# Transposing DMA transfers for the second layer's keys of three heads, in place of turning them on TensorE

## The chip, the cores and the metric

One core of one Trainium2 chip. The metric is the device time of the whole kernel in microseconds (us). Runs of one kernel lie within about 0.8% here; a verdict of "faster" or "slower" needs 2%. A ratio is the mean time of one kernel's fast runs over the mean of the other's fast runs of the same rounds, so it is not quite the ratio of the medians that are quoted. Profiles are single executions. The runs below were made in three batches, each on another chip and beside before, whose medians there were 1132.5, 1131.1 and 1134.4 us; a difference between runs of two batches is good to a few us only.

## The reference, cut to what matters

Two identical layers of cached attention and an MLP, for 8 batch rows with one new token each. Each layer reads the same caches.

```python
def _A_ref(x, k_cache, v_cache, wq, wo):          # caches: (8, 8, 4096, 256), bf16
    q = (x @ wq).reshape(B, 1, 16, 256)...        # 16 query heads on 8 key heads
    scores = einsum("bhqd,bhkd->bhqk", q, k) * 256 ** -0.5
    o = einsum("bhqk,bhkd->bhqd", softmax(scores), v)
    return o... @ wo
x = x + _A_ref(_layernorm(x), ...)    # layer 1
x = x + _B_ref(_layernorm(x), ...)    # MLP
x = x + _A_ref(_layernorm(x), ...)    # layer 2, the same caches
x = x + _B_ref(_layernorm(x), ...)
```

One head of one batch row has 2 MB of keys and 2 MB of values. A score needs the sum over the 256 dimensions. The kernel's matmuls take the keys with the dimensions on the partitions, and the cache has them the other way round: the keys have to be turned (transposed).

## The kernel before

A small planner in the kernel, run when the kernel is built, orders all work over the engines and issues all loads on one queue, that of SyncE (SP). SBUF holds 30 quarters of 512 KB for keys and values. Of each batch row the keys of five "kept" heads stay in SBUF from layer 1 to layer 2; the three "free" heads (0, 1, 2) are loaded and turned again in layer 2. That makes 64 + 24 = 88 fresh key heads.

A load, four quarters at most, and the turning of half a quarter on TensorE, pairs of bf16 taken as one f32, with the eviction back into the same place:

```python
src = cache[b, h].rearrange("(m s) d -> m (s d)", m=P)[:, u * 2048:(u + n) * 2048]
dst = kv[:, q * 2048:(q + n) * 2048]
o.emit = lambda eng: eng.dma_start(dst, src)
# ... cut ...
def transpose_piece(i, pc):
    # ... 4 transposes of 128x128 f32 into a PSUM bank ...
    last = t.transpose(psT[bank][:, s * P:(s + 1) * P], src, ident_f[:, :])
    # ... then one copy back by VectorE or ScalarE, whichever the planner picks
```

After it the key of pair c (even or odd dimensions) lies at every second element, and the queries are made for even and odd dimensions to match:

```python
w = wq_sb[:, kc, hq * 256 + c:hq * 256 + 256:2]          # queries
a = slot_ap(q, s * 256, 256)                             # scores, 16 per quarter
last = t.matmul(ps[:, 2 * i:2 * i + 2 * REP], a[:, c:256:2], bcast(rhs(c), REP, 1), ...)
```

The planner's constants for a load are its rate and `ISSUE`, the time from issue to its start.

Of the kernel before, what the change touches and what calls it, by code (L numbers as in the profile page):

```python
# [6 lines left out]
P = 128  # L7
# [16 lines left out]
REP = 24  # L24
AT = (-4, -3, -2)
MLP_AT = 3
MIX = "KKKKKFFF"
QFIRST = 1
PV0 = 0
PV1 = PV0 + DH  # L30
QW, HW, YW = 24, 24, 12
SC = 448
# [30 lines left out]
class Plan:  # L63
# [3 lines left out]
    WIN, COLS, TARGET = 3.413, 3000, 3500  # L67


    ISSUE, LEAD = 3.5, 6.0  # L70
    BLOCK, FETCH = 128, 6.0
    LAT = {"pe": 0.25, "dve": 0.06, "act": 0.06, "pool": 0.05, "sp": 0.4}

# [364 lines left out]
def bass_interleave_layers__gqa_block_cached__mixer_s_mlp__decode_kernel(  # L438
# [38 lines left out]
    wq_sb = sb("wq_sb", [P, 3, 4096], bf)  # L477
# [86 lines left out]


    FASTER = 1.05

    def dma(name, dst, src, nbytes, sem, val, wr, at, row=8192):

# [11 lines left out]

    def issue_kv(o, n, q):

        (cache, b, h), u = o.unit.tile, o.unit.u
        src = cache[b, h].rearrange("(m s) d -> m (s d)", m=P)[:, u * 2048:(u + n) * 2048]
        dst = kv[:, q * 2048:(q + n) * 2048]
        slot_n[q] += 1
        o.emit = lambda eng: eng.dma_start(dst, src)
        o.dma = (slot_sem[q], 16 * slot_n[q])
        o.dur = ((n << 15) / 26.88e3 + 8 * 0.008) / FASTER  # L590

    plan.issue_kv = issue_kv

    def load(cache, b, h, units, keep=()):

        out = {}
        tile = (cache, b, h)
        for u in units:
            x = out[u] = Unit(tile, u, u in keep)
            o = plan.op("sp", None, 0.0, "kv", wr=[("s", x, 0), ("s", x, 1)], prio=loads[0])  # L600
            o.unit = x
            loads[0] += 1
        return out
# [54 lines left out]
    def pe(fn, n, rd=(), wr=(), banks=(), name="chain", prio=None, pairs=None):  # L658
        if prio is None:
            prio = urge[0] + len(plan.ops)  # L660
        d = 0.06 + 0.026 * n
        return plan.op("pe", fn, (d, d, 20 * n, pairs or n), name, rd=rd, wr=wr, banks=banks, prio=prio)
# [86 lines left out]
               rd=["xc", "rsy"], wr=["base"])  # L749
            dv(lambda v: v.tensor_tensor(bs, bs, src, ALU.add), rd=["base", skey], wr=["base"])  # L750

    def q_mms(t, mts, rhs, bank, at, step, copies):



        last = None
        for i, mt in enumerate(mts):
            hq, c = mt // 2, mt % 2
            for kc in range(4):


                if kc < 3:
                    w = wq_sb[:, kc, hq * 256 + c:hq * 256 + 256:2]
                    r = rhs(kc)
                else:
                    o = (hq % 8) * 256
                    w = wqx_sb[:, o + c:o + 256:2]
                    r = rhs(3 + hq // 8)
                if step == 1:
                    r = bcast(r, copies, 1)  # L770
                last = t.matmul(bank[:, at + i * step:at + i * step + copies], w, r,  # L771
                                start=(kc == 0), stop=(kc == 3))
        return last
# [20 lines left out]
    def column_sums():  # L794

        def one(kc):
            return mask[:, kc:kc + 1]
        for g in range(4):
            pe(lambda t, g=g: q_mms(t, range(8 * g, 8 * g + 8), one, psM, SC, 1, QW), 32,
               rd=["mask"] + WQ, wr=["psM"], banks=[M], prio=len(plan.ops))  # L800

            dv(lambda v, g=g: v.tensor_copy(
                cs_q[:, 8 * g:8 * g + 8].rearrange("p (h c j) -> p h c j", c=2, j=2),
                psM[:, SC:SC + 8].rearrange("p (h j c) -> p h c j", c=2, j=2)),
               rd=["psM"], wr=["cs_q"], banks=[M], prio=len(plan.ops))
        pe(lambda t: h_mms(t, one, psM, SC, 1, HW), 56, rd=["mask"] + W3, wr=["psM"], banks=[M],
           prio=len(plan.ops))
        dv(lambda v: v.tensor_copy(cs_h[:, :], psM[:, SC:SC + 14]), rd=["psM"], wr=["cs_h"], banks=[M],
           prio=len(plan.ops))
# [72 lines left out]
    def front(layer, b, h):  # L882


        g = fronts[0]
        fronts[0] += 1
        par, nr, nm = 0, free_p.pop(0), g % NS
        ps, bk = psS, "S"
        kept_k, kept_v = state.pop((0, b, h)) if layer else ({}, {})
        keep_k = KEPT_K.get(h, ()) if layer == 0 else ()  # L890
        if layer == 0:
            def rhs(c):
                return q1T[:, b, 4 * h + 2 * c:4 * h + 2 * c + 2]
            qk = [("q1T", 0), ("q1T", 1)]
        else:
            def rhs(c):
                return q2T[b % 2][:, 4 * h + 2 * c:4 * h + 2 * c + 2]
            qk = [("q2", b, h)]
        ks = dict(kept_k)
        fresh = [u for u in range(4) if u not in ks]  # L900
        ks.update(load(A_k_cache, b, h, fresh, keep_k))
        for u in range(4):
            if u in fresh:
                for pc in range(2):
                    transpose_piece(ks[u], pc)

            def sc(t, u=u, q=ks[u]):
                last = None
                for s in range(8):
                    i = 8 * u + s  # L910


                    for c in range(2):
                        a = slot_ap(q, s * 256, 256)
                        last = t.matmul(ps[:, 2 * i:2 * i + 2 * REP], a[:, c:256:2],  # L915
                                        bcast(rhs(c), REP, 1), start=(c == 0), stop=(c == 1))
                return last
            o = plan.op("pe", sc, (0.022 * 16 + 0.06, 32 * REP / 1200 + 0.01, 32 * REP, 16), "sc",
                    rd=qk + [("s", ks[u], 0), ("s", ks[u], 1)],
                    wr=[("sc", par, x) for x in range(u, 4)], banks=[bk])  # L920
            if u not in keep_k:
                o.frees = ks[u]
        hi = len(plan.ops) - 10 ** 5
        scs = [("sc", par, x) for x in range(4)]

        ss = sS[nm]
        plan.op("dve", lambda v: v.tensor_copy(ss[:, :], ps[:, 0:64]), 0.17, "max", rd=scs,  # L927
                wr=[("sS", nm)], banks=[bk], prio=hi)
        sview = ss[:, :].rearrange("p (i j) -> p j i", j=2)
        plan.op("dve", lambda v: v.tensor_reduce(pm[nm][:, :], sview, axis=AX.X, op=ALU.max), 0.23,  # L930
                "max", rd=[("sS", nm)], wr=[("pm", nm)], prio=hi)
        plan.op("pool", lambda gp: gp.partition_all_reduce(gm[nm][:, :], pm[nm][:, :], P, RO.max),  # L932
                0.46, "max", rd=[("pm", nm)], wr=[("gm", nm)], prio=hi)
        plan.op("dve", lambda v: v.tensor_single_scalar(nb[nm][:, :], gm[nm][:, :], -INV_SQRT_DH,  # L934
                                                        ALU.mult), 0.15, "max",
                rd=[("gm", nm)], wr=[("nb", nm)], prio=hi)

        for jj in range(2):
            def ex(a, jj=jj):
                return a.activation(pT[nr][:, :, :].rearrange("p i j -> p j i")[:, jj, :],  # L940
                                    sview[:, jj, :], ACT.Exp, bias=nb[nm][:, jj:jj + 1],
                                    scale=INV_SQRT_DH, accum_out=rs[nr][:, jj:jj + 1])
            plan.op("act", ex, 0.5, "exp", rd=[("nb", nm), ("sS", nm)], wr=[("pT", nr, jj), ("rs", nr, jj)], prio=hi)
        plan.op("pool", lambda gp: gp.partition_all_reduce(Db[nr][:, :], rs[nr][:, :], P, RO.add),  # L944
                0.5, "sum", rd=[("rs", nr, 0), ("rs", nr, 1)], wr=[("Db", nr)], prio=hi)
        plan.op("dve", lambda v: v.reciprocal(rc[nr][:, :], Db[nr][:, :]), 0.15, "sum",
                rd=[("Db", nr)], wr=[("rc", nr)], prio=hi)
        state[layer, b, h] = ({u: ks[u] for u in keep_k}, kept_v, nr)
# [160 lines left out]
    def second_queries(b, h, prio):  # L1109

        q, src = q2T[b % 2], x2c[b % 2]
        pe(lambda t: q_mms(t, range(4 * h, 4 * h + 4), lambda kc: src[:, kc, 0:1], psM, SC,
                           1, QW), 16, rd=[("x2", b)] + WQ, wr=["psM"], banks=[M], prio=prio)
        dv(lambda v: v.scalar_tensor_tensor(
            q[:, 4 * h:4 * h + 4].rearrange("p (c j) -> p c j", c=2),
            psM[:, SC:SC + 4].rearrange("p (j c) -> p c j", c=2), rsy[:, 0, 0:1],
            t_q[:, 4 * h:4 * h + 4].rearrange("p (c j) -> p c j", c=2), ALU.mult, ALU.add),
           rd=["psM", "rsy", "t_q"], wr=[("q2", b, h)], banks=[M], prio=prio)
# [25 lines left out]
    def first_queries():  # L1144
# [9 lines left out]
           banks=[M])  # L1154
        norm(xT[:, :, :], "xT", False)
        for h in range(8):
            pe(lambda t, h=h: q_mms(t, range(4 * h, 4 * h + 4), lambda kc: yb[:, kc, :], psM,
                                    32 * h, B, B), 16, rd=YB + WQ, wr=["psM"], banks=[M])
        for c in range(2):
            dv(lambda v, c=c: v.tensor_copy(  # L1160
# [129 lines left out]
```

## Time and profile before

| | us |
|---|---|
| median of 3 runs | 1135.38 (1130.73 to 1138.06) |
| profiled span | 1124.7 |
| bytes from HBM | 446.8 MB |

Lines of the page of before: busy time by engine, GB/s in 40 equal slices of the span, the kernel's DMA queue (packets, MB, share of 16 engines' span), the chain that ended last, and the groups that turn and evict keys (line, engine, operation, tiles, count, busy us, mean ns of one, idle before and what ended it):

```profile
PE 959.9 (85%) x19455; PEld 771.8 (69%) x19455; DVE 556.0 (49%) x1749; ACT 275.8 (25%) x839; POOL 98.0 (9%) x273
GB/s 334 408 424 421 389 397 424 422 421 382 419 425 423 415 379 422 423 425 408 393 425 423 421 387 409 423 425 420 371 412 426 424 417 374 426 420 398 365 336 132
q1 hardware_dynamic: 59392, 446.80, 97.5%
...
PE 53%; DMA 35%; DVE 5%; issue 5%; SPq 1%; POOL 0%; ACT 0%
...
L1067 PE MATMUL psT<-ident_f,kv 128*128 128x128 f32 x2816 | 398.4, 288 | 32.1 <-DMA kv<-in_A_k_cache_dram 28.9
L1075 DVE COPY kv<-psT 128x512 f32<-128x512 f32 x388 | 267.1, 691 | 214.9 <-PE psT L1067 213.9
L1076 ACT COPY kv<-psT 128x512 f32<-128x512 f32 x316 | 184.9, 586 | 407.6 <-PE psT L1067 407.6
```

Three stretches of before by window (start and end in us, length, busy time and count of each engine (PE, its weight loads, VectorE, ScalarE, GpSimd), granted TensorE clock as a share of full speed, busy share of the DMA engines, GB/s): normal streaming, one batch row's MLP chain, and the tail.

```profile
169.00:253.00 84.00, 75.27 (x1298) 63.80 (x1297) 44.00 (x112) 29.33 (x81) 7.96 (x21) 0.94 1.00 422
267.00:281.00 14.00, 10.78 (x263) 6.69 (x261) 7.41 (x42) 0.21 (x1) 0.00 (x0) 0.98 0.97 352
1054.00:1110.00 56.00, 46.88 (x1072) 39.01 (x1069) 25.77 (x94) 11.83 (x43) 6.05 (x16) 0.88 0.90 331
```

How to read it: in the long stretch the DMA engines are busy all the time and deliver 422 GB/s; TensorE is busy 75 of 84 us, close behind. At 424 GB/s the traffic alone takes 449.5 MB / 424 GB/s = 1060 us. The remaining 65 us are the head, a dip in each batch row (352 GB/s here, where the MLP's serial chain runs and loads come in quarters) and the tail. The chain gives TensorE 53%: both are loaded, and the chain alone doesn't tell which one sets the rate.

### The profile page before, as it was taken

How to read it: one execution, taken by the hardware profiler on the slowest of the kernel's cores; microseconds unless marked ns; L12 is line 12 of the kernel's file. 1: busy time of each engine (PE TensorE's matmuls, PEld its weight loads, DVE VectorE, ACT ScalarE, POOL GpSimd, SP SyncE). 2: the span in 40 equal slices, each digit the busy share in tenths (PEclk: the TensorE clock that was granted, in tenths of full speed). 3: DMA queues.
4: the chain of work that ended last, by engine and by line, in shares of the span. 5: the costliest groups of instructions: out<-in, count | busy, mean ns of one | idle time of the engine just before them, and what ended most of it. 6: DMA issues, size and time to landing. Idle time of an engine off the chain costs nothing.

```text
span 1124.7 us, 42351 instructions
## 1 busy us (share of the span) xinstructions
PE 959.9 (85%) x19455; PEld 771.8 (69%) x19455; DVE 556.0 (49%) x1749; ACT 275.8 (25%) x839; POOL 98.0 (9%) x273
## 2 busy tenths in 40 slices
PE   5888888898789989798898987989878988898887
PEld 4677557785678757687677855777666975676775
DVE  4345435455365544454455543655534554456444
ACT  1133012341123302243023411233012430132120
POOL 0001010010100101010010101001010010110010
PEclk9899899899899999999899998899999999999888
DMA  9999999999999999999999999999999999999993
GB/s 334 408 424 421 389 397 424 422 421 382 419 425 423 415 379 422 423 425 408 393 425 423 421 387 409 423 425 420 371 412 426 424 417 374 426 420 398 365 336 132
DMA packets 59570, 449.50 MB, mean 400 GB/s; under 512 B 6384, under 2 KB 9600, under 8 KB 34688
## 3 DMA queue, kind: packets, MB, share of 16 engines
q1 hardware_dynamic: 59392, 446.80, 97.5%
q8 instruction: 152, 2.49, 0.9%
q14 instruction: 26, 0.21, 0.0%
HBM read 446.77 MB, written 0.01 MB: 397 GB/s over the span
## 4 chain that ended last, share of the span: by engine, by line
PE 53%; DMA 35%; DVE 5%; issue 5%; SPq 1%; POOL 0%; ACT 0%
DMA kv<-in_A_k_cache_dram 23%; PE psT L1067 21%; PE psS L915 15%; DMA kv<-in_A_v_cache_dram 11%; PE psP L970 8%; PE psR L1017 3%; PE psM L771 2%; PE psT L1231 1%; DVE oS L982 1%; DVE oS L984 1%; DMA w3x_sb<-in_B_w_dram 1%; PE psP L992 1%; PE psM L868 1%; PE psM L871 1%; SPq L571 1%
## 5 line engine op out<-in xcount | busy, mean ns | idle before, releaser
L1067 PE MATMUL psT<-ident_f,kv 128*128 128x128 f32 x2816 | 398.4, 288 | 32.1 <-DMA kv<-in_A_k_cache_dram 28.9
L1075 DVE COPY kv<-psT 128x512 f32<-128x512 f32 x388 | 267.1, 691 | 214.9 <-PE psT L1067 213.9
L1067 PEld LDWEIGHTS psT<-ident_f,kv 128*128 128x128 f32 x2816 | 320.2, 147 | 54.2 <-DMA kv<-in_A_k_cache_dram 35.4
L1076 ACT COPY kv<-psT 128x512 f32<-128x512 f32 x316 | 184.9, 586 | 407.6 <-PE psT L1067 407.6
L970 PE MATMUL psP<-kv,pT 128*2 128x256 bf16 x4096 | 168.2, 278 | 26.0 <-DMA kv<-in_A_v_cache_dram 15.1
L940 ACT ACTIVATE pT<-sS,nb 128x32 bf16<-128x32 f32 x256 | 81.7, 326 | 332.1 <-DVE nb L934 332.0
L915 PE MATMUL psS<-q2T,kv 128*128 128x48 bf16 x4096 | 141.9, 187 | 20.2 <-issue 19.3
L915 PEld LDWEIGHTS psS<-q2T,kv 128*128 128x128 bf16 x4096 | 126.3, 99 | 44.0 <-issue 39.4
L915 PEld LDWEIGHTS psS<-q1T,kv 128*128 128x128 bf16 x4096 | 136.9, 98 | 14.4 <-issue 9.6
L915 PE MATMUL psS<-q1T,kv 128*128 128x48 bf16 x4096 | 145.7, 184 | 0.9 <-issue 0.9
L970 PEld LDWEIGHTS psP<-kv,pT 128*2 128x2 bf16 x4096 | 79.2, 82 | 63.9 <-issue 25.9
L932 POOL PARTITION_ALL_REDUCE gm<-pm x128 | 45.6, 356 | 792.2 <-DVE pm L930 792.2
L927 DVE COPY sS<-psS 128x64 f32<-128x64 f32 x128 | 28.7, 224 | 120.7 <-PE psS L915 116.3
L992 PE MATMUL psP<-sel,oS 128*128 128x2 bf16 x512 | 32.2, 166 | 48.6 <-DVE oS L984 44.0
L982 DVE CAST oS<-psP 128x256 bf16<-128x256 f32 x128 | 53.9, 421 | 38.7 <-PE psP L970 35.6
L992 PEld LDWEIGHTS psP<-sel,oS 128*128 128x128 bf16 x512 | 24.4, 99 | 68.4 <-DVE oS L984 62.8
L1017 PE MATMUL psR<-wo_sb,oT 128*1 128x448 bf16 x448 | 65.4, 375 | 5.1 <-DVE oT L998 4.9
L944 POOL PARTITION_ALL_REDUCE Db<-rs x128 | 51.2, 400 | 202.2 <-ACT pT L940 202.2
L984 DVE TENSOR_TENSOR oS<-psP,oS 128x256 bf16<-128x256 f32 x128 | 54.2, 423 | 3.2
L1231 PE MATMUL psT<-ident_b 128*128 128x512 bf16 x162 | 54.4, 416 | 0.0
L940 ACT ACTIVATION_READ_ACCUMULATOR pT<-sS,nb 128x1 f32 x256 | 48.1, 188 | 0.0
L771 PEld LDWEIGHTS psM<-x2c,wq_sb 128*128 128x128 bf16 x768 | 30.3, 98 | 21.7 <-issue 17.1
(126 smaller groups left out, 505.7 us busy)
## 6 DMA issues: line engine op xcount, KB each, us to landing
kv<-in_A_k_cache_dram SPq DMA_DIRECT2D x71, 2048.0 KB, 21.7
kv<-in_A_v_cache_dram SPq DMA_DIRECT2D x51, 2048.0 KB, 19.2
kv<-in_A_v_cache_dram SPq DMA_DIRECT2D x171, 512.0 KB, 7.6
kv<-in_A_v_cache_dram SPq DMA_DIRECT2D x42, 1024.0 KB, 12.1
kv<-in_A_k_cache_dram SPq DMA_DIRECT2D x9, 1536.0 KB, 16.0
kv<-in_A_v_cache_dram SPq DMA_DIRECT2D x7, 1536.0 KB, 15.0
kv<-in_A_k_cache_dram SPq DMA_DIRECT2D x21, 512.0 KB, 8.8
kv<-in_A_k_cache_dram SPq DMA_DIRECT2D x10, 1024.0 KB, 14.5
```

The source lines that it names most:

```text
L771: last = t.matmul(bank[:, at + i * step:at + i * step + copies], w, r, start=(kc == 0), stop=(kc == 3))
L915: last = t.matmul(ps[:, 2 * i:2 * i + 2 * REP], a[:, c:256:2], bcast(rhs(c), REP, 1), start=(c == 0), stop=(c == 1))
L940: return a.activation(pT[nr][:, :, :].rearrange("p i j -> p j i")[:, jj, :], sview[:, jj, :], ACT.Exp, bias=nb[nm][:, jj:jj + 1], scale=IN ...
L970: last = t.matmul(ps[g4:g4 + 2, PV0:PV0 + DH], pT[nr][:, i, :], slot_ap(q, s * 256, 256), start=(i < 4), stop=(i >= 28), skip_group_check= ...
L982: plan.op("dve", lambda v: v.tensor_copy(oS[:, 0, :], po), 0.36, "o", rd=[("pv", par, x) for x in range(4)], wr=["oS0"], banks=[bk], prio=hi)
L984: plan.op("dve", lambda v: v.tensor_tensor(oS[:, 1, :], po, oS[:, 0, :], ALU.subtract), 0.36, "o", rd=["oS0"] + [("pv", par, x) for x in r ...
L992: last = t.matmul(ps[:, PV1 + 2 * c:PV1 + 2 * c + 2], oS[:, w, c:DH:2], sel[:, :], start=(w == 0), stop=(w == 1))
L1017: last = t.matmul(psR[r:r + 1, 0:D], oT[no][:, i % 2, i // 2:i // 2 + 1], wo_sb[:, a:a + D], start=(k == 1 and i < 2), stop=(k == HKV - 1 ...
L1067: last = t.transpose(psT[bank][:, s * P:(s + 1) * P], src, ident_f[:, :])
L1075: return e.tensor_copy(dst, psT[bank][:, :])
L1076: return e.copy(dst, psT[bank][:, :])
L1231: return t.matmul(psT[bank][:, :], ident_b[:, :], bcast(ident_b[:, :], 4, 1), start=True, stop=True)
```

## The change

Intent: take the turning of 24 of the 88 key heads (layer 2, heads 0 to 2 of all 8 batch rows) off TensorE, VectorE and ScalarE and let the DMA engines turn them on their way in. The transposing transfer is given blocks of 128 elements of 2 bytes (256 bytes), so the first 128 dimensions and the last 128 lie in separate blocks; the queries of these heads are made in halves instead of even and odd dimensions.

```diff
+TURNED = {(1, 0), (1, 1), (1, 2)}
-    ISSUE, LEAD = 3.5, 6.0
+    ISSUE, LEAD = 4.0, 6.0
+    TURN_RATE = 24.5e3                       # the planner's rate, bytes per us and engine
 def issue_kv(o, n, q):
+        if turned:
+            dst = dst.rearrange("p (c m) -> p c m", m=P)
+            o.emit = lambda eng: eng.dma_start_transpose(dst, src)
+            o.dur = (n << 15) / TURN_RATE / FASTER
 def q_mms(...):
+                p = slice(128 * c, 128 * c + 128) if (layer, hq // 2) in TURNED else slice(c, 256, 2)
 def front(layer, b, h):
-            if u in fresh:
+            if u in fresh and not turned:
                 ... transpose_piece(ks[u], pc)
-                        last = t.matmul(ps[...], a[:, c:256:2], ...)
+                        a = a[:, 128 * c:128 * c + 128] if turned else a[:, c:256:2]
+                        last = t.matmul(ps[...], a, ...)
```

More of the change, by code (lines that the diff above doesn't have):

```diff
@@ L582, in issue_kv @@
     def issue_kv(o, n, q):
-        (cache, b, h), u = o.unit.tile, o.unit.u
+        (cache, b, h, turned), u = o.unit.tile, o.unit.u
         src = cache[b, h].rearrange("(m s) d -> m (s d)", m=P)[:, u * 2048:(u + n) * 2048]
@@ L587, in issue_kv, with load @@
         slot_n[q] += 1
-        o.emit = lambda eng: eng.dma_start(dst, src)
         o.dma = (slot_sem[q], 16 * slot_n[q])
-        o.dur = ((n << 15) / 26.88e3 + 8 * 0.008) / FASTER
+        if turned:
+            dst = dst.rearrange("p (c m) -> p c m", m=P)
+            o.emit = lambda eng: eng.dma_start_transpose(dst, src)
+            o.dur = (n << 15) / TURN_RATE / FASTER
+        else:
+            o.emit = lambda eng: eng.dma_start(dst, src)
+            o.dur = ((n << 15) / 26.88e3 + 8 * 0.008) / FASTER
     plan.issue_kv = issue_kv
-    def load(cache, b, h, units, keep=()):
+    def load(cache, b, h, units, keep=(), turned=False):
         out = {}
-        tile = (cache, b, h)
+        tile = (cache, b, h, turned)
         for u in units:
@@ L750, in norm, with q_mms @@
             dv(lambda v: v.tensor_tensor(bs, bs, src, ALU.add), rd=["base", skey], wr=["base"])
-    def q_mms(t, mts, rhs, bank, at, step, copies):
+    def q_mms(t, layer, mts, rhs, bank, at, step, copies):
         last = None
@@ L759, in q_mms @@
             for kc in range(4):
+                p = slice(128 * c, 128 * c + 128) if (layer, hq // 2) in TURNED else slice(c, 256, 2)
                 if kc < 3:
-                    w = wq_sb[:, kc, hq * 256 + c:hq * 256 + 256:2]
+                    w = wq_sb[:, kc, hq * 256:hq * 256 + 256][:, p]
                     r = rhs(kc)
@@ L766, in q_mms @@
                     o = (hq % 8) * 256
-                    w = wqx_sb[:, o + c:o + 256:2]
+                    w = wqx_sb[:, o:o + 256][:, p]
                     r = rhs(3 + hq // 8)
@@ L798, in column_sums @@
         for g in range(4):
-            pe(lambda t, g=g: q_mms(t, range(8 * g, 8 * g + 8), one, psM, SC, 1, QW), 32,
+            pe(lambda t, g=g: q_mms(t, 1, range(8 * g, 8 * g + 8), one, psM, SC, 1, QW), 32,
                rd=["mask"] + WQ, wr=["psM"], banks=[M], prio=len(plan.ops))
@@ L900, in front @@
         fresh = [u for u in range(4) if u not in ks]
-        ks.update(load(A_k_cache, b, h, fresh, keep_k))
+        turned = (layer, h) in TURNED
+        ks.update(load(A_k_cache, b, h, fresh, keep_k, turned))
         for u in range(4):
-            if u in fresh:
+            if u in fresh and not turned:
                 for pc in range(2):
@@ L914, in sc @@
                         a = slot_ap(q, s * 256, 256)
-                        last = t.matmul(ps[:, 2 * i:2 * i + 2 * REP], a[:, c:256:2],
+                        a = a[:, 128 * c:128 * c + 128] if turned else a[:, c:256:2]
+                        last = t.matmul(ps[:, 2 * i:2 * i + 2 * REP], a,
                                         bcast(rhs(c), REP, 1), start=(c == 0), stop=(c == 1))
@@ L1111, in second_queries @@
         q, src = q2T[b % 2], x2c[b % 2]
-        pe(lambda t: q_mms(t, range(4 * h, 4 * h + 4), lambda kc: src[:, kc, 0:1], psM, SC,
+        pe(lambda t: q_mms(t, 1, range(4 * h, 4 * h + 4), lambda kc: src[:, kc, 0:1], psM, SC,
                            1, QW), 16, rd=[("x2", b)] + WQ, wr=["psM"], banks=[M], prio=prio)
@@ L1156, in first_queries @@
         for h in range(8):
-            pe(lambda t, h=h: q_mms(t, range(4 * h, 4 * h + 4), lambda kc: yb[:, kc, :], psM,
+            pe(lambda t, h=h: q_mms(t, 0, range(4 * h, 4 * h + 4), lambda kc: yb[:, kc, :], psM,
                                     32 * h, B, B), 16, rd=YB + WQ, wr=["psM"], banks=[M])
```

## The prediction

> **What bounds the kernel now.** The DMA engines. The page's slices show them busy in tenths of 9 almost to the end, and its queue part gives the kernel's queue 97.5% of 16 engines' span, for 446.8 MB. In stretches without serial work (windows from 169 to 253 us, for instance) they deliver 422 to 426 GB/s at a DMA share of 1.00 to 1.02, while PE is busy 12 to 13 of 14 us. At 424 GB/s the traffic takes about 1060 us; the other 65 us are the head (325 to 343 GB/s for 28 us), one dip per batch at the MLP chain (346 to 373 GB/s, share 0.93 to 1.01, quarter transfers of 512 KB in a row) and the tail (330 to 370 GB/s from 1054 us, 262 from 1097, nothing in the last 14 us). PE (85% busy) is close behind; the chain of waits, PE 53% and DMA 35%, shows that both are loaded, not that PE sets the rate.
>
> **What the change removes.** 24 of 88 fresh key heads (layer two, heads 0 to 2, 8 batches) lose their turning on TensorE: 768 of 2816 f32 transposes, about 109 of 398 us of PE's busy time (groups by line), and 192 of 704 evictions, about 123 of 452 us on DVE and ACT.
>
> **What it adds.** The same 50.3 MB come through transposing transfers, 42 of them (12 of 2 MB, 14 of 512 KB), on the same queue. Plain, at 621 ns per 16 KB packet, a head takes all engines 5.0 us, together 120 us. The Trainium skill, "Advanced Engine Details and Errata", section X-Bar Transpose (TRN2), expects 350 to 400 GB/s; "DMA: Bandwidth & Descriptors", section Latency and other measured facts, has 261 GB/s for a source that is not contiguous. No trace here shows a turned transfer yet. The kernel's constant of 24.5 bytes per ns and engine is 392 GB/s: 128 us, 8 more than now. At 350 it is 24 more, at 261 it is 73. These are estimates from the skill.
>
> **How much lies on the critical path.** The relieved heads run in stretches that are DMA-bound at 424 GB/s already, so most of PE's 109 us is worth nothing. The dips come from the chain's latency and the few free quarters, which don't change. A gain is likely in the tail, where three such heads of the last batch are turned with the DMA below its rate: 5 to 9 us. Fewer quarter transfers (170 of 512 KB instead of 192; a 4 KB packet takes 173 ns, a quarter of a 16 KB one 155) are worth 3 us.
>
> **Sum.** 1135 plus 8 (likely) to 25 for the turned transfers, less about 10: about 1136 us, range 1112 to 1180. Faster by over 2%: 0.12; within 2%: 0.58; slower by over 2%: 0.30.
>
> **What would show it.** Right: PE busy about 850 us, evictions about 330; DMA share still 97% or more; in stretches with turned heads GB/s below 424 at a share of 1.00; layer-one stretches unchanged; the tail several us shorter. Wrong: stretches with turned heads still at 424 (turning free: about 1122 us), or far below it with the DMA idle between transfers (the issuing engine held by each turned transfer).
>
> **What would make it wrong.** A source of 256-byte pieces with 16 KB between rows that runs at 261 GB/s or less; turned transfers that don't overlap with plain ones before and after, a gap for each of the 42; or earlier freed quarters that fill the dips, which could bring 20 us more than I expect.

## The result, and the profile after

| | before | after |
|---|---|---|
| median of 3 runs, us | 1135.38 | 1256.57 (1251.93 to 1260.42) |
| ratio of fast runs | | 1.1071, 95% interval 1.0988 to 1.1155 |
| profiled span, us | 1124.7 | 1250.1 |

Slower by 10.7%, far outside the range of 1112 to 1180.

The lines of the page of after that answer to those of before, with the two counters that are new (packets by size, and HBM bytes read):

```profile
PE 952.8 (76%) x18824; PEld 713.8 (57%) x18824; DVE 478.3 (38%) x1622; ACT 239.9 (19%) x774; POOL 98.0 (8%) x273
GB/s 345 410 424 402 371 284 367 424 418 359 267 396 424 401 318 271 426 421 363 337 273 425 422 382 293 342 426 420 365 271 371 425 412 376 336 290 408 222 305 189
DMA packets 249307, 449.41 MB, mean 359 GB/s; under 512 B 203424, under 2 KB 206640, under 8 KB 227120
q1 hardware_dynamic: 249136, 446.80, 102.5%
HBM read 396.44 MB, written 0.01 MB: 317 GB/s over the span
...
DMA 44%; PE 41%; SPq 6%; issue 4%; DVE 4%; POOL 0%; ACT 0%
...
L1079 PE MATMUL psT<-ident_f,kv 128*128 128x128 f32 x2048 | 280.1, 283 | 6.6 <-DMA kv<-in_A_k_cache_dram 4.5
L1087 DVE COPY kv<-psT 128x512 f32<-128x512 f32 x261 | 180.2, 691 | 147.6 <-PE psT L1079 147.4
L1088 ACT COPY kv<-psT 128x512 f32<-128x512 f32 x251 | 147.3, 587 | 312.1 <-PE psT L1079 312.1
L1243 PE MATMUL psT<-ident_b 128*128 128x512 bf16 x299 | 111.0, 472 | 0.0
```

Three things stand out. The transposes are gone as planned: 2816 became 2048, 398.4 us became 280.1, and the evictions fell from 452.0 to 327.5 us. TensorE's busy time still fell only from 959.9 to 952.8 us: the fillers that the planner puts into idle time and means to hold TensorE's clock with (L1243; its name for them is `warm`) rose from 162 (54.4 us) to 299 (111.0 us), and values and scores ran longer, at a granted clock of 0.85 against 0.945. And the GB/s line now has a hole in every batch row, down to between 267 and 293, and to 222 in the last.

Windows of after, over the first batch row's three turned heads: each turned transfer from its first to its last packet, then the whole stretch, then a stretch of layer 1 behind it.

```profile
160.30:173.50 13.20, 7.96 (x207) 5.87 (x204) 3.45 (x15) 1.44 (x8) 1.51 (x4) 0.87 1.29 214
178.40:187.20 8.80, 2.68 (x52) 1.61 (x52) 1.34 (x6) 0.72 (x4) 0.40 (x1) 0.57 1.34 262
192.60:200.80 8.20, 4.55 (x57) 1.80 (x54) 1.66 (x7) 0.72 (x4) 0.76 (x2) 0.92 1.28 283
160.30:200.80 40.50, 21.03 (x448) 13.77 (x445) 7.06 (x31) 2.88 (x16) 3.02 (x8) 0.78 1.21 278
211.00:253.00 42.00, 37.67 (x644) 30.90 (x643) 21.68 (x54) 15.03 (x40) 3.79 (x10) 0.97 1.01 425
```

In the turned transfers the DMA engines are busy all the time (a share over 1 means that the packets' times overlap) and deliver 214 to 283 GB/s, values that travel beside them included. Before and behind, the rate is what it was.

The packet records show what a turned transfer is made of. Each 2 MB head comes as 8192 packets of 256 bytes, 196,608 in all (24 x 8192), at a median of 18 ns each, where a plain packet of 16 KB takes 614 ns (64 x 18 ns would be 1152, if they did not overlap). No run parts the turning from the size of these packets: no plain transfer was cut into 256-byte packets. The records of before suggest that the size alone could do it: its plain packets of 896, 1792, 4096 and 16384 bytes have medians of 41, 76, 159 and 614 ns, and the straight line through the first and the last would give a packet of 256 bytes 17 ns (an estimate).

To see where the span went, I took from these records, microsecond by microsecond, the part of each by which the rate lay under 424 GB/s, and summed it by stretch (us; the head and the final chain are included, what lies before the first load is not; the 1000 us are counted from the first record, about 11 us ahead of the span; a microsecond in which a turned transfer begins or ends counts as inside it):

```
kernel                                         in turned    elsewhere,    elsewhere,
                                               transfers    first 1000    rest
before with ISSUE 4.0 (run below)                 0.0          32.5         26.4
after with plain transfers (the plain twin)       0.0          38.6         20.4
after                                           124.2          39.5         25.5
```

So nearly the whole loss lies in the turned transfers themselves: 124.2 / 24 = 5.2 us of all DMA engines for each head.

### The profile page after: what moved, and what is told of

Same layout as the page of the kernel before. It is cut to its first block, busy times and chain, and to the rows that moved or that the text cites. A ratio compares the mean times of both kernels' runs of the same rounds, so it can differ in the third digit from the quotient of the medians.

```text
span 1250.1 us, 40850 instructions
## 1 busy us (share of the span) xinstructions
PE 952.8 (76%) x18824; PEld 713.8 (57%) x18824; DVE 478.3 (38%) x1622; ACT 239.9 (19%) x774; POOL 98.0 (8%) x273
## 3 DMA queue, kind: packets, MB, share of 16 engines
HBM read 396.44 MB, written 0.01 MB: 317 GB/s over the span
## 4 chain that ended last, share of the span: by engine, by line
DMA 44%; PE 41%; SPq 6%; issue 4%; DVE 4%; POOL 0%; ACT 0%
DMA kv<-in_A_v_cache_dram 24%; DMA kv<-in_A_k_cache_dram 18%; PE psT L1079 12%; PE psS L927 11%; PE psP L982 8%; SPq L594 5%; PE psT L1243 3%; PE psR L1029 2%; PE psM L781 2%; SPq L597 1%; DMA w3x_sb<-in_B_w_dram 1%; DVE oS L994 1%; DVE oS L996 1%; PE psM L878 1%; PE psP L1004 1%
## 5 line engine op out<-in xcount | busy, mean ns | idle before, releaser
L1079 PE MATMUL psT<-ident_f,kv 128*128 128x128 f32 x2048 | 280.1, 283 | 6.6 <-DMA kv<-in_A_k_cache_dram 4.5
L982 PE MATMUL psP<-kv,pT 128*2 128x256 bf16 x4096 | 191.4, 310 | 98.4 <-DMA kv<-in_A_v_cache_dram 93.1
L1079 PEld LDWEIGHTS psT<-ident_f,kv 128*128 128x128 f32 x2048 | 228.9, 145 | 24.9 <-DMA kv<-in_A_k_cache_dram 14.3
L1087 DVE COPY kv<-psT 128x512 f32<-128x512 f32 x261 | 180.2, 691 | 147.6 <-PE psT L1079 147.4
L1088 ACT COPY kv<-psT 128x512 f32<-128x512 f32 x251 | 147.3, 587 | 312.1 <-PE psT L1079 312.1
L927 PEld LDWEIGHTS psS<-q2T,kv 128*128 128x128 bf16 x4096 | 134.3, 104 | 112.3 <-DMA kv<-in_A_k_cache_dram 72.8
L1243 PE MATMUL psT<-ident_b 128*128 128x512 bf16 x299 | 111.0, 472 | 0.0
L1029 PE MATMUL psR<-wo_sb,oT 128*1 128x448 bf16 x448 | 74.7, 421 | 10.8 <-DVE oT L1010 6.3
L1004 PE MATMUL psP<-sel,oS 128*128 128x2 bf16 x512 | 32.3, 167 | 52.2 <-DVE oS L996 52.0
L1010 DVE TENSOR_TENSOR oT<-psP,rc 128x4 bf16<-128x4 f32 x128 | 20.5, 160 | 112.9 <-PE psP L1004 109.4
L1243 PEld LDWEIGHTS psT<-ident_b 128*128 128x128 bf16 x299 | 26.5, 108 | 44.3 <-issue 38.6
## 6 DMA issues: line engine op xcount, KB each, us to landing
wq_sb<-in_A_wq_dram SPq DMA_DIRECT2D x3, 1024.0 KB, 16.8
```

The costliest lines, as they stand in the source:

```text
L927: last = t.matmul(ps[:, 2 * i:2 * i + 2 * REP], a, bcast(rhs(c), REP, 1), start=(c == 0), stop=(c == 1))
L982: last = t.matmul(ps[g4:g4 + 2, PV0:PV0 + DH], pT[nr][:, i, :], slot_ap(q, s * 256, 256), start=(i < 4), stop=(i >= 28), skip_group_check= ...
L1004: last = t.matmul(ps[:, PV1 + 2 * c:PV1 + 2 * c + 2], oS[:, w, c:DH:2], sel[:, :], start=(w == 0), stop=(w == 1))
L1029: last = t.matmul(psR[r:r + 1, 0:D], oT[no][:, i % 2, i // 2:i // 2 + 1], wo_sb[:, a:a + D], start=(k == 1 and i < 2), stop=(k == HKV - 1 ...
L1087: return e.tensor_copy(dst, psT[bank][:, :])
L1088: return e.copy(dst, psT[bank][:, :])
```

## The experiments

### 1. Loads alone

A kernel that only loads, with seven phases, each awaited to the end; it gives zeros. Phases A and B differ in this:

```diff
-    return eng.dma_start(dst, src)                                            # plain
+    return eng.dma_start_transpose(dst.rearrange("p (c m) -> p c m", m=P), src)   # turned
```

Phase D takes as source the head as 8192 rows of 256 bytes that follow one another: `cache[b, h].rearrange("k (c d) -> (k c) d", d=P)`.

> A kernel of loads alone, which gives zeros on purpose. Seven phases, each awaited to the end: A six plain heads of 2 MB; B six turned heads of 2 MB; C six turned heads in 24 quarters; D six turned heads whose source rows of 256 bytes follow one another; E three turned and three plain heads in turn on one queue; F three turned heads from the SP queue beside three plain ones from the ACT queue; G three turned heads, each awaited alone. Theory 1, the DMA engines themselves turn slowly: A about 31 us (424 GB/s), B 50 to 66 us (8.5 to 11 us a head, as in the trace of after) with the engines busy all the time, F about the sum of its parts, 40 to 48 us, E the same. Theory 2, the issuing queue is the limit (it is held 13 us by a turned head): in B the engines are busy well under 80%, and F takes about as long as its turned part alone, 26 to 33 us. Theory 3, the source pitch of 16 KB is the limit: D takes 31 to 37 us [...] where B takes 50 or more. If turning were only slow beside other work of the kernel, B would take 32 to 38 us.

The seven phases A to G by window (of G its first head):

```profile
1.80:32.70 30.90, 0.00 (x0) 1.00 0.98 407
34.60:84.90 50.30, 0.00 (x0) 1.00 1.13 250
86.80:153.10 66.30, 0.00 (x0) 1.00 1.06 190
155.00:203.90 48.90, 0.00 (x0) 1.00 1.21 257
205.40:247.20 41.80, 0.00 (x0) 1.00 1.12 301
248.80:289.40 40.60, 0.00 (x0) 1.00 1.09 310
291.30:299.70 8.40, 0.00 (x0) 1.00 1.11 250
```

- A: six plain heads 30.9 us. B: six turned heads 50.3 us, 250 GB/s, 8.4 us a head, share 1.13. Nothing else ran, so the slowness belongs to the transfer. A single awaited head (G) takes 8.4 us too.
- C: quarters are slower still, 66.3 us: (66.3 - 50.3) / 18 further transfers = 0.89 us for each.
- D: a contiguous source helps by 3% (48.9 us). My guess that the 16 KB between the rows costs the rate falls. Its packets are of 256 bytes too, so it says nothing of their size.
- F: three turned heads from SP and three plain ones from ScalarE's queue take 40.6 us, exactly the sum of their parts (3 x 8.4 + 30.9 / 2 = 40.6). So the two kinds share one resource and don't overlap, and it isn't the issuing queue. E, the same on one queue, takes 41.8, 0.4 us more for each pair (single executions). In the trace of after, each whole turned head holds the queue 13 to 19 us:

```profile
152.83 17.87 SPq L594 DMA_TRANSPOSE kv<-in_A_k_cache_dram  x1
170.75 1.15 SPq L597 DMA_DIRECT2D kv<-in_A_v_cache_dram  x1
171.95 13.65 SPq L594 DMA_TRANSPOSE kv<-in_A_k_cache_dram  x1
185.64 0.58 SPq L597 DMA_DIRECT2D kv<-in_A_v_cache_dram  x1
```

These long holds look like the cause and aren't: while SP stands in one, the DMA engines are working through what it issued before.

### 2. The same plan with plain transfers, and the constants alone

`e_plain_same_plan`, the plain twin, keeps the plan of after, its order, sizes and slots, and replaces the transposing transfers by plain ones. Its scores of 24 heads are wrong.

```diff
-            o.emit = lambda eng: eng.dma_start_transpose(dst, src)
+            o.emit = lambda eng: eng.dma_start(kv[:, q * 2048:(q + n) * 2048], src)
```

> After with its turned transfers replaced by plain ones of the same slots, sizes and places in the queue, and everything else as it is; the result is wrong on purpose (the keys of 24 heads stay unturned). It parts the price of the transposing transfer from the worth of the PE and eviction time that the change takes away. Theory 1 and 2 (the transfer is what costs): 1110 to 1135 us, 120 to 145 us under after; the taken-away PE time is worth 0 to 25 us against before, mostly in the tail. A rival, that the new plan and order of loads costs the time: 1200 us or more.

Measured: 1122.48 us (1120.18 to 1124.20), 0.9908 of before (0.9881 to 0.9935). The transposing transfer alone is worth 1256.6 - 1122.5 = 134 us, and the new plan is not at fault. Its page and the window that matches the turned stretch of after:

```profile
PE 918.4 (82%) x18824; PEld 705.7 (63%) x18824; DVE 477.7 (43%) x1622; ACT 239.9 (21%) x774; POOL 97.6 (9%) x273
GB/s 332 409 425 422 376 403 424 424 420 387 395 425 424 423 368 418 424 425 418 352 423 427 422 405 391 425 424 424 366 395 424 425 422 386 397 421 421 382 408 170
```

```profile
160.30:200.80 40.50, 29.12 (x613) 18.18 (x611) 11.15 (x44) 3.60 (x20) 3.77 (x10) 0.87 1.01 427
```

The same 40.5 us move 427 instead of 278 GB/s, and TensorE is busy only 29 of them. This is also the measured upper bound of the change: if turning in the DMA were free, it would bring 0.9%. (The correctness check passed this kernel, although three of eight heads of layer 2 have scores from unturned keys. The check doesn't see these wrong scores, so that a turned version passes proves little.)

`e_issue_only` is before with the change's other constant alone:

```diff
-    ISSUE, LEAD = 3.5, 6.0
+    ISSUE, LEAD = 4.0, 6.0
```

> Before with the change's other constant alone, ISSUE 4.0 instead of 3.5 us. All theories: within 1% of before, 1125 to 1145 us; if it were part of the loss it would show 10 us or more.

Measured: 1124.37 us, 0.9939 (0.9903 to 0.9975). Most of the bound above is therefore this constant: between 1124.4 and 1122.5 us there is no difference outside the noise. Taking away about 118 us of TensorE's transposes and 124 us of evictions brought nothing that these runs can tell from noise.

`e_issue45`, with 4.5:

> Before with ISSUE 4.5 us, to see whether the small gain of 4.0 (0.6%) goes on. Expected 1118 to 1132 us; no theory of the turned transfers depends on it.

Measured: 1128.87 us, 0.9976 (0.9928 to 1.0024). The gain doesn't go on. Before with ISSUE 4.0 is the best correct kernel, by 0.6%; its interval excludes 1.

### 3. The planner told the truth

The planner believed 24.5 bytes per ns and engine for a turned transfer.

```diff
-    TURN_RATE = 24.5e3
+    TURN_RATE = 12.0e3
```

> After with the planner told 12 bytes per ns and engine for a turned transfer (what the trace shows: 2 MB in about 10.5 us) instead of 24.5. Rival theory (the plan is bad because its constant is wrong): at least 40 us of the 121 come back, 1215 us or less. Theory 1: the engines' time stays, so 1235 to 1260 us.

Measured: 1242.47 us, 1.0962 (1.0931 to 1.0992). It gives back 14 of 121 us (12 by the ratios, whose intervals just overlap). The wrong constant is a small part at most.

### 4. Whole heads only, and one head instead of three

A turned head took 8.4 us alone but 10.5 (median, first to last packet) in after. My reason was the splitting: after moves 24 heads in 42 transfers. `e_whole` lets the planner wait until four neighbouring quarters are free (with 12 bytes per ns as above):

```diff
+            whole = u.tile[3]
+            if whole and not any(k >= 4 for k, a in runs(max(free["sp"], times[-1]))):
+                return None
-            for t in [max(free["sp"], times[0])] + [x for x in times if free["sp"] < x <= late]:
+            for t in [...] + [x for x in times if free["sp"] < x and (x <= late or whole)]:
```

> After with the planner told 12 bytes per ns and engine, and a turned head never split: 24 transfers of 2 MB instead of 42. Theory 'the engines' own turning rate plus a fixed cost of each transfer': 24 heads at 8.4 to 9 us instead of 5.0 are 80 to 95 us over the plain twin's 1122 us, so 1205 to 1225 us. Rival 'the queue is held by long turned transfers': wholes hold it longest, so no better than the 1242 us of the run with the rate alone told, 1240 or more.

Measured: 1246.58 us, 1.1025 (1.0983 to 1.1066). A miss: I expected 1205 to 1225. No split was left, and its 24 transfers still took 10.3 us each (247.3 us in all). The run with the rate alone told had 31 turned transfers, this one 24, and it is no faster: fewer splits bring no gain here. It is what the rival foresaw, too, but the table in experiment 6 shows why the rival's reason, the held queue, doesn't follow: the loss stays inside the transfers, where the engines work, and not between them.

`e_whole_one` is the same with `TURNED = {(1, 0)}`, 8 heads in all.

> The same with one turned head of each batch instead of three. If each turned head costs the same 3.4 to 4 us of DMA time, 8 heads cost 27 to 32 us over the plain 1122 to 1124 us: 1149 to 1157 us, a third of the loss of the whole-head kernel with three. If a stall sets in at the first turned transfer of each batch whatever their number: 1180 us or more. If one head could hide in slack: 1120 to 1135.

Measured: 1166.90 us, 1.0325 (1.0294 to 1.0357). A miss too: I expected 1149 to 1157. Over the plain twin that is 44.4 us for 8 heads, 5.5 each; with three heads in each row (`e_whole`) it is 124.1 for 24, 5.2 each (5.9 and 5.3 by the ratios). The loss grows with the number of heads, and each is dearer by 1.8 to 2.1 us than loads alone explain (8.4 - 5.0 = 3.4).

### 5. Why a head takes 10.3 us in the kernel and 8.4 alone

A second kernel of loads alone tried three suspects.

> Loads alone again, zeros on purpose, to find why a head took 8.4 us alone in the first loads kernel but 10.5 us (median) in after. A six turned heads in 12 halves of 1 MB; B six turned heads beside a stream of matmuls; C six plain heads beside the same; D six turned heads beside copies on VectorE; E three times one turned head and then one plain head in quarters of 512 KB. Theory 'each turned transfer has its own fixed cost' (24 quarters took 66.3 us where 6 wholes took 50.3, 0.89 us for each further transfer): A 55 to 57 us, B and D 50 to 51. Theory 'work of the compute engines slows the crossbar writes': A about 50 to 57, B or D 58 us or more, with C still 31. Theory 'plain quarters behind it slow it': E clearly over its sum of 25.2 + 16 = 41 us, 46 or more.

Its phases A to E by window:

```profile
4.10:59.10 55.00, 0.00 (x0) 0.00 (x0) 0.00 (x0) 0.00 (x0) 1.00 1.04 229
61.00:114.30 53.30, 53.30 (x242) 23.96 (x241) 0.00 (x0) 0.00 (x0) 1.00 1.14 237
127.80:159.10 31.30, 31.30 (x147) 14.18 (x145) 0.00 (x0) 0.00 (x0) 1.00 0.97 403
167.30:218.80 51.50, 0.00 (x0) 0.00 (x0) 40.36 (x59) 0.00 (x0) 0.52 1.15 245
220.90:264.60 43.70, 0.00 (x0) 0.00 (x0) 0.00 (x0) 0.00 (x0) 0.50 1.09 288
```

Halves (A) cost 55.0 us, 0.8 us for each further transfer, as expected. Matmuls beside it (B, 53.3 us) and VectorE copies (D, 51.5 us) cost little, if more than the 50 to 51 that I expected, and quarters behind turned heads (E) take 43.7, 3 over the sum. None of these makes the missing 1.9 us a head. But B's 3.0 us over the 50.3 of loads alone had a pattern in the packet records: B had two instruction fetches (packets of 16 KB on a queue whose kind the profile names `instruction`), and behind each about 20 of the 256-byte packets took around 1.3 us instead of 18 ns. The same was there in the whole-head kernel. One such place, at 932.5 us of `e_whole`, as starts of 256-byte packets on all engines in steps of 200 ns, counted from 32 ns behind the start of a fetch that took 960 ns:

```
from us   0.0  0.2  0.4  0.6  0.8  1.0  1.2  1.4  1.6  1.8  2.0
packets   213  213   26    0    3    7    7    8   99  229  226
```

For about a microsecond nearly all of them stop, not one in sixteen, though the fetch is a single packet. If one engine alone had been held, about 200 packets of each step would have gone on. The turned transfers of the whole-head kernel hold 35 such fetches (30 of 16 KB and 5 of 8 KB), those of after 34.

The third kernel of loads alone tests it: many short instructions on TensorE (A, B), and on three engines (C, D), beside six turned heads (A, C) or six plain ones (B, D).

> Loads alone, zeros on purpose, beside many short instructions, so that the engines' instruction memories are filled again and again by fetches (16 KB each, on the same DMA engines). A six turned heads beside short matmuls, B six plain heads beside half as many, C six turned heads beside short work on three engines, D six plain heads beside half of that. In the traces of after and of the whole-head kernel nearly every fetch inside a turned transfer goes with some 20 packets that take 1.3 us instead of 0.018. Theory 'a turned transfer runs in lockstep on all 16 engines, so one fetch on one engine stops all': A and C take 50.3 us plus about 1.0 to 1.4 us for each fetch (with 8 fetches in A 58 to 62 us, with 20 in C 70 or more), while B and D stay within 1 to 2 us of 30.8. Rival 'it was something else in the kernel': A and C 50 to 53 us whatever the number of fetches.

```profile
2.80:61.20 58.40, 26.53 (x958) 25.99 (x955) 0.00 (x0) 0.00 (x0) 0.00 (x0) 1.00 1.22 218
63.10:95.40 32.30, 12.68 (x465) 12.46 (x462) 0.00 (x0) 0.00 (x0) 0.00 (x0) 1.00 0.94 389
97.40:157.00 59.60, 26.31 (x955) 25.84 (x952) 59.23 (x979) 36.03 (x387) 0.00 (x0) 1.00 1.24 214
159.20:193.20 34.00, 12.96 (x471) 12.68 (x467) 29.37 (x486) 17.78 (x191) 0.00 (x0) 1.00 0.91 373
```

A had 8 fetches of 16 KB and took 58.4 us: (58.4 - 50.3) / 8 = 1.0 us for each. The packet records say that it is the fetches and not the short matmuls: behind every one of the 8 the starts of packets fall under a third of the usual rate for 1.2 to 1.5 us, and 173 packets took over 0.7 us; in the same phase without fetches, B of the first loads kernel, not one did. C had 7 of 16 KB and 11 smaller ones of 8 KB on a further queue and took 59.6; the "70 or more" that I had said for 20 full fetches was not put to the test, as there were fewer. The plain phases with 4 fetches of 16 KB each took 32.3 (B) and 34.0 us (D; 6 small ones too), 1.4 and 3.1 over the 30.9 of loads alone. That is more than the "1 to 2 us" I had set for D, but B's price for each fetch is 0.4 us against 1.0. In a phase of only six transfers one late engine can set the end, so the price of a fetch in a long plain stream is not measured here.

With it the sum for a turned head of `e_whole` nearly closes. The records lose 122.5 / 24 = 5.1 us a head. Its own rate makes 3.4. For the fetches I summed the steps of 100 ns behind each in which fewer than a third of the usual packets start: 31.8 us for 35 fetches, 0.9 us each, in line with the 1.0 of the test, and 1.3 us a head (after: 30.7 us for 34). That leaves 0.4. Such slow steps are also found in the first 2 us of the transfers, 29.6 us in all, while the end of the plain transfer ahead is still coming in; as plain bytes move then, only a part of it is lost. That the remaining 0.4 us are this part is argued, not shown.

### 6. The last batch row alone

If turning by DMA pays anywhere, then in the tail, where DMA runs at 331 GB/s in before. `e_last_batch` turns the three heads of the last row only; its queries keep even and odd dimensions, so these scores are wrong.

```diff
-        turned = (layer, h) in TURNED
+        turned = (layer, h) in TURNED and b == B - 1
```

> Turning by DMA in the last batch alone, in the tail, where PE and its evictions are nearest to being the limit; the planner is told 12 bytes per ns. The queries keep the interleaved halves of before, so the scores of these three heads are wrong on purpose; the time is not touched by that. Theory: three heads cost 3 x 5.2 us of DMA time, less what the tail gains (my prediction said 5 to 9 us; the plain twin suggests 0 to 4): 1127 to 1140 us. A rival, that turning pays where PE is the limit: 1118 or less.

Measured: 1136.02 us, 1.0035 (0.9990 to 1.0080): 11.6 us over before with ISSUE 4.0 (10.9 by the ratios, as the two were run in different batches) and inside the 1127 to 1140 expected. The table of lost microseconds for all kernels, as above:

```
kernel              in turned    elsewhere,    elsewhere,    sum     profiled
                    transfers    first 1000    rest                  span
e_issue_only           0.0          32.5         26.4        58.9     1120.8
e_plain_same_plan      0.0          38.6         20.4        59.0     1120.0
e_last_batch          16.4          36.1         18.3        70.8     1131.9
e_whole_one           42.8          35.5         23.8       102.1     1162.7
e_whole              122.5          36.7         25.8       185.0     1246.1
after                124.2          39.5         25.5       189.2     1250.1
```

The span less the sum is 1060.6 to 1061.9 us in all six: the bytes at 424 GB/s. The tail does gain, 8.1 us in `e_last_batch` and 6.0 in the plain twin, but 16.4 us go into the three turned transfers, and part of the gain is given back in the dips of earlier rows (38.6 against 32.5 in the twin). Why these dips grow with the new plan was not followed up.

## Why the prediction was wrong

- **"The DMA engines bound the kernel": right.** The plain twin takes a quarter of the transposes and evictions away and gains 0.9%, most of it from another constant.
- **"The relieved heads run in stretches that are DMA-bound, so most of PE's 109 us is worth nothing": right.** Between the twin and `e_issue_only` there are 2 us; by the table, 6 gained in the tail and 6 lost in the dips of earlier rows.
- **The step that failed: "The kernel's constant of 24.5 bytes per ns and engine is 392 GB/s: 128 us, 8 more than now".** No trace showed a turned transfer, and I took a constant of the kernel's planner as the likely rate, because it agreed with the 350 to 400 GB/s of the Trainium skill ("Advanced Engine Details and Errata", section X-Bar Transpose (TRN2)). Alone on the queue it is 250 GB/s: 24 x (8.4 - 5.0) = 82 us in place of 8. I had the right figure as the bad case ("at 261 it is 73") and gave it no room: 1135 + 73 - 10 is 1198, outside my own range.
- **Not in the sum at all:** a turned transfer stops nearly as a whole when an instruction fetch holds it up, about 1 us each, some 31 us in after. It was read from packets of the same size that suddenly take 70 times as long, which only the trace of a turned transfer could show. The 82 and the 31 make 113 of the 124.2 us lost in the turned transfers of after; the other 11 were not parted (18 further transfers by splitting, slow starts).
- **"A source of 256-byte pieces with 16 KB between rows": half right.** It runs in 256-byte packets, but a contiguous source is hardly faster (257 against 250 GB/s). Whether the size of the packets or the turning makes the rate was not tested.
- **"Far below it with the DMA idle between transfers (the issuing engine held)", "a gap for each of the 42": wrong as a cause.** The engine is held, but the DMA works meanwhile; all loss lies inside the transfers.
- **"The tail, 5 to 9 us": the mechanism is right.** 6 to 8 us by the records.
- **"PE busy about 850 us": wrong.** 952.8: the transposes fell by 118 us as foreseen, but the planner filled the longer idle time with 137 more warming matmuls (56.6 us), and the clock granted was lower. The evictions (327.5 against 330) and the 170 transfers of 512 KB (154 + 2 plain and 14 turned) came as foreseen.

## What to carry to other kernels

When the DMA engines bound a kernel, work that is moved onto them has to be paid there in full, however slow the engine is that it came from: ask first what the relieved engine's time is worth (here a twin with free transfers gave 0.9%), and then what the transfer takes alone on the queue. A rate that stands as a constant in a kernel is not a measurement; a ten-line kernel of loads alone gives one. And look at packet sizes and outliers in the DMA records: the same bytes, turned and in 256-byte packets, cost 1.6 times the plain price here, and the outliers led to the rest.

## What the Trainium skill lacked or had wrong

- "Advanced Engine Details and Errata", section X-Bar Transpose (TRN2): it says that transposing transfers are as fast as regular ones and expects 350 to 400 GB/s. Measured alone: 250 GB/s in transfers of 2 MB, 190 in 512 KB, against 407 for plain ones in the same kernel.
- "DMA: Bandwidth & Descriptors", section Latency and other measured facts: its 261 GB/s for a source that isn't contiguous is near the measured 250; its 350 to 400 for the contiguous case is not what a contiguous source gave here, 257.
- "VectorE: DVE Perf Modes", section The three transpose paths, has the crossbar at about 90% of DMA bandwidth; here it was 250 / 407 = 61%.
- "DMA: Bandwidth & Descriptors", section Rules for kernel authors, says that spreading DMAs over issuing engines doesn't help, as all run on the same 16 engines. This case agrees, for turned beside plain too: 40.6 us from two queues, the sum of the parts.
- No page that I read has the price of an instruction fetch inside a turned transfer, about 1.0 us of the whole transfer (8 fetches, 58.4 - 50.3 us), nor that of each further transposing transfer, 0.8 to 0.9 us.
- No page that I read says that the profile's HBM counter leaves turned reads out: 396.44 MB of 446.8 in after, short by the 50.3 MB that were turned (and by 16.8 MB in `e_whole_one`, its 8 heads).
